# Grouped attention on one core: score columns laid out in whole PSUM banks, 12 score matmuls per group in place of 18

One core of one Trainium2 chip. The metric is the device time of one execution, in microseconds (us); the median of several executions is quoted.

## The reference

```python
B, Hq, Hkv, Sq, Sk, D = 16, 32, 8, 288, 512, 128          # bf16 inputs, values 0.05 * normal
k = jnp.repeat(k, Hq // Hkv, axis=1); v = jnp.repeat(v, Hq // Hkv, axis=1)
scores = jnp.einsum("bhqd,bhkd->bhqk", q, k) * D ** -0.5
p = softmax(scores, axis=-1)
out = jnp.einsum("bhqk,bhkd->bhqd", p, v)
```

Four query heads share one key/value head. The kernel treats each of the 16 x 8 = 128 pairs of batch and key head as a **group**: 4 x 288 = 1152 query rows are nine tiles of 128, and 512 keys are four tiles of 128, so a group has 36 score tiles of 128 x 128.

## The kernel before

A group is worked in three **chunks** of three query tiles, 1536 score columns each, three banks of PSUM. Two chunk buffers take turns (`ps_s`), the exponentials go to six buffers in SBUF (`pt_sb`). For chunk n TensorE computes scores, ScalarE takes the exponential without subtracting a maximum (a check at the end falls back to a general path), and TensorE multiplies chunk n-3's exponentials with V, to which a column of ones is appended that gives the row sums. VectorE divides. In every ninth chunk VectorE computes the last 120 columns of the exponential itself (a "shared" chunk).

```python
BANK, TPC = 512, 3                 # TPC: query tiles per chunk
CH = TPC * BANK                    # 1536
LAG, W, EVERY, FIRST_SHARED = 3, 120, 9, 4
TW = TPC * P                       # 384: one key tile's columns within a chunk

cuts = sorted(set(range(0, CH + 1, BANK)) | set(range(0, CH + 1, TW)))
pieces = [(c, c // TW, c % TW, e - c) for c, e in zip(cuts[:-1], cuts[1:])]   # 384,128,256,256,128,384

def op_s(n):                       # scores of chunk n
    g, i = n // NC, n % NC
    waits = [have("k", g), have_q(g, i)]
    if n >= 2:
        waits.append(("s_e", n - 1))              # exponential n-2 has freed the buffer
    qg = qt_sb[:, g % NQ, i * TPC:(i + 1) * TPC].rearrange("d t p -> d (t p)")
    for x, (c, j, r0, w) in enumerate(pieces):
        if shared(n) and c + w == CH:
            w -= W
        ... matmul(ps_s[:, n % 2, c:c + w], kt_sb[:, sl, j, gi, :], qg[:, r0:r0 + w])

def op_pv(r):                      # values of chunk r
    waits = [("s_vc", g + 1), ("s_e", r + 1)] ...
    for j in range(NJ):
        for a in range(TPC):
            ... matmul(outs(r)[:, a, :], pt_sb[:, r % NPT, j, a * P:(a + 1) * P], v_sb[...])

# TensorE:
for n in range(NS):                # NS = 384
    op_s(n)
    ...
    if n >= LAG:
        op_pv(n - LAG)
```

The start: the first group's queries come in three transposing loads of three tiles, the first K is loaded plainly, transposed by TensorE and copied in one piece; dummy matmuls fill TensorE's time until then.

Of the kernel before, what the change touches and what calls it, by code (L numbers as in the profile page):

```python
# [131 lines left out]
def bass_standalone__gqa_softmax__near_ridge_kernel(  # L132
# [8 lines left out]
    P = 128  # L141
# [20 lines left out]
    W = 120  # L162
    EVERY = 9
    NB = 2
    TW = TPC * P
    UG = 4
    NU = NG // UG
    NSLOT = 3
    NQ = 12
    NPT = 6  # L170
    WARM = 5
    FIRST_SHARED = 4
    AHEAD = 1.08
    NO = 12
    NS = NG * NC
# [10 lines left out]
    with ExitStack() as es:  # L186
# [20 lines left out]
            S("s_q%d" % i)  # L207
        for i in range(NO):
            S("s_o%d" % i)
        for i in range(NC):  # L210
            S("s_qp%d" % i)


# [24 lines left out]
        ident = main.enter_context(nc.sbuf_tensor("ident", [P, P], BF16))  # L238
        ones_b = main.enter_context(nc.sbuf_tensor("ones_b", [P, P], BF16))
        kt_sb = main.enter_context(nc.sbuf_tensor("kt_sb", [P, NSLOT, NJ, UG, P], BF16))  # L240
        pt_sb = main.enter_context(nc.sbuf_tensor("pt_sb", [P, NPT, NJ, TW], BF16))
        o_sb = main.enter_context(nc.sbuf_tensor("o_sb", [P, NO, NT, D], BF16))
        rl_sb = main.enter_context(nc.sbuf_tensor("rl_sb", [P, NG * NT], FP32))
        st_sb = main.enter_context(nc.sbuf_tensor("st_sb", [P, 2, B], FP32))
# [25 lines left out]
        def emit(eng, waits, fn):  # L270
            waits = need(eng, waits)
            for (s, n) in waits[:-1]:
                eng.wait_ge(s, n)
            ins = fn()
            if waits:
                ins.wait_op(waits[-1][0], waits[-1][1], "sem-ge")
            return ins
# [33 lines left out]

        def op_q0(i):

            c0, c1 = i * TPC, (i + 1) * TPC
            nc.sync.dma_start_transpose(qt_sb[:, 0, c0:c1], q_v[0:P, c0 * D:c1 * D]).then_inc(sem["s_qp%d" % i], 16)  # L315

        def have_q(g, i):
            if g == 0:
                return ("s_qp%d" % i, 16)
            return ("s_q%d" % (g % NQ), 16 * (g // NQ + (0 if g % NQ == 0 else 1)))  # L320

        def have(kind, g):

            u = g // UG
            if u == 0 and kind == "k":
                return ("s_k%d" % min(g, 2), (1, 1, 16)[min(g, 2)])
            if u == 0:
                return ("s_v%d" % (g // 2 * 2), 16)
            return ("us_%s%d" % (kind, u % NSLOT), 16 * (u // NSLOT + (0 if u % NSLOT == 0 else 1)))
# [16 lines left out]



        cuts = sorted(set(range(0, CH + 1, BANK)) | set(range(0, CH + 1, TW)))
        pieces = [(c, c // TW, c % TW, e - c) for c, e in zip(cuts[:-1], cuts[1:])]  # L350

        def op_kt(g, tiles, bank):

# [19 lines left out]
        def op_s(n):  # L373
            eng = nc.tensor
            g, i = n // NC, n % NC
            sl, gi = (g // UG) % NSLOT, g % UG
            waits = [have("k", g), have_q(g, i)]
            if n >= 2:
                waits.append(("s_e", n - 1))
            qg = qt_sb[:, g % NQ, i * TPC:(i + 1) * TPC].rearrange("d t p -> d (t p)")  # L380
            for x, (c, j, r0, w) in enumerate(pieces):
                if shared(n) and c + w == CH:
                    w -= W
                ins = emit(eng, waits if x == 0 else [], lambda: eng.matmul(  # L384
                    ps_s[:, n % 2, c:c + w], kt_sb[:, sl, j, gi, :], qg[:, r0:r0 + w], start=True, stop=True))
                if n == 0 and c + w == BANK:
                    ins.then_inc(sem["s_s0"], 1)
            ins.then_inc(sem["s_s"], 1)

        def op_sy(n):  # L390

            eng = nc.tensor
            g, t = n // NC, n % NC * TPC + TPC - 1
            emit(eng, [("s_ev", n - LAG - 1)], lambda: eng.matmul(  # L394
                ps_o[:, (n - LAG) % 2, BANK - W:BANK], kt_sb[:, (g // UG) % NSLOT, NJ - 1, g % UG, :],
                qt_sb[:, g % NQ, t, P - W:P], start=True, stop=True))

        def outs(r):

            if r == NS - 1:  # L400
                return ps_s[:, (NS - 2) % 2].rearrange("p (a e) -> p a e", e=BANK)[:, :, 0:DV]
            return ps_o[:, r % 2, 0:TPC * DV].rearrange("p (a e) -> p a e", e=DV)

        def op_pv(r):
            eng = nc.tensor
            g = r // NC
            sl, gi = (g // UG) % NSLOT, g % UG
            waits = [("s_vc", g + 1), ("s_e", r + 1)]
            if 2 <= r < NS - 1:
                waits.append(("s_ev", r - 1))  # L410


            for j in range(NJ):
                for a in range(TPC):
                    w_x = waits if a == 0 and j == 0 else []
                    if a == TPC - 1 and j == NJ - 1 and shared(r):
                        w_x = w_x + [("s_yp", nth(r))]
                    ins = emit(eng, w_x, lambda: eng.matmul(  # L418
                        outs(r)[:, a, :], pt_sb[:, r % NPT, j, a * P:(a + 1) * P],
                        v_sb[:, sl, gi * NJ + j, 0:DV], start=(j == 0 and a == 0), stop=(j == NJ - 1),  # L420
                        skip_group_check=True))
            ins.then_inc(sem["s_pv"], 1)

        def op_pv_last(a):

            eng = nc.tensor
            sl, gi = (LASTG // UG) % NSLOT, LASTG % UG
            for j in range(NJ):
                ins = emit(eng, [("s_e", NS + (0 if a < TPC - 1 else 1))], lambda: eng.matmul(
                    outs(NS - 1)[:, a, :], pt_sb[:, (NS - 1) % NPT, j, a * P:(a + 1) * P],  # L430
                    v_sb[:, sl, gi * NJ + j, 0:DV], start=(j == 0), stop=(j == NJ - 1)))
            if a == TPC - 1:
                ins.then_inc(sem["s_pv"], 1)


        def op_exp(n):
            eng = nc.scalar
            waits = [("s_s", n + 1)]
            if n >= NPT:
                waits.insert(0, ("s_pv", n - NPT + 1))  # L440
            dst, src = pt_sb[:, n % NPT], ps_s[:, n % 2].rearrange("p (j r) -> p j r", r=TW)
            parts = [(dst.rearrange("p j r -> p (j r)"), ps_s[:, n % 2])]
            if shared(n):
                parts = [(d[:, 0:CH - W], s[:, 0:CH - W]) for (d, s) in parts]
            if n == 0:
                d, s = parts[0]
                emit(eng, [("s_s0", 1)], lambda: eng.activation(d[:, 0:BANK], s[:, 0:BANK], ACTF.Exp, scale=scale))  # L447
                parts = [(d[:, BANK:CH], s[:, BANK:CH])]
            if n == NS - 1:
                w = TW - P  # L450
                parts = [(dst[:, :, 0:w], src[:, :, 0:w]), (dst[:, :, w:TW], src[:, :, w:TW])]
            for (d, s) in parts:
                emit(eng, waits, lambda: eng.activation(d, s, ACTF.Exp, scale=scale)).then_inc(sem["s_e"], 1)  # L453


        def shared(n):
            return FIRST_SHARED <= n < NS - 6 and (n - FIRST_SHARED) % EVERY == 0

        def nth(n):
            return (n - FIRST_SHARED) // EVERY + 1  # L460

# [27 lines left out]

        def op_yp(n):  # L490
            eng, b = nc.vector, nth(n) % NB
            emit(eng, [("s_pv", n - NPT + 1), ("s_ym", 2 * nth(n)), ("s_yu", 3 * nth(n))],
                 lambda: eng.scalar_tensor_tensor(  # L493
                     out=pt_sb[:, n % NPT, NJ - 1, TW - W:TW], in0=u_sb[:, b, 2], scalar=QUARTIC[3],
                     in1=e_sb[:, b].bitcast(FP32), op0=ALU.add, op1=ALU.mult)).then_inc(sem["s_yp"], 1)


# [62 lines left out]
                op0=ALU.is_lt, op1=ALU.add)).then_inc(sem["s_bad"], 1)  # L560


        first = [lambda i=i: op_q0(i) for i in range(NC)]
        first += [lambda: op_q(1), lambda: op_k(0, 2), lambda: op_q(2), lambda: op_v(0, None, 2, UG), lambda: op_q(3)]

        sp = []
# [21 lines left out]
        @block.tensor  # L588
        def _(eng):
            op_warm(WARM, BANK, ps_o[:, 1])  # L590
            op_kt(0, range(NJ), 0)
            op_warm(8, P, ps_s[:, 1])
            for n in range(NS):
                if n == 2:
                    op_warm(4, P, ps_o[:, 0])
                op_s(n)
                if shared(n):
                    op_sy(n)
                if n == 2:
                    op_kt(1, range(NJ), 1)  # L600
                if n >= LAG:
                    op_pv(n - LAG)
            for r in range(NS - LAG, NS - 1):
                op_pv(r)
            for a in range(TPC):
                op_pv_last(a)
            emit(eng, [("s_ev", NS - 1), ("s_bad", 2)], lambda: eng.matmul(  # L607
                ps_o[0:1, NS % 2, 0:ALONE + 1], one_f[:], bad_sb[:, 1, :], start=True, stop=True)
            ).then_inc(sem["s_bad"], 1)
            choose(eng, "pe")  # L610
# [26 lines left out]
        def _(eng):  # L637
            eng.memset(z_sb[:], 0.0).then_inc(sem["s_z"], 1)  # L638
            eng.memset(dum[:], 0.0).then_inc(sem["s_one"], 1)
            eng.memset(one_f[:], 1.0)  # L640
            op_kc(0, range(NJ), 0, 1)
            op_kc(1, range(NJ), 1, 2)
            per_b = G * NC
            w0 = NS - 1 - ALONE // TPC
            last = rl_sb[:, NG * NT - ALONE:NG * NT]
# [62 lines left out]
```

## Time and profile before

| | before |
|---|---|
| time, median | 525.38 us (525.32 to 526.12, 3 runs) |
| span in the profile | 523.5 us |
| TensorE busy, ScalarE busy | 99%, 98% |
| score matmuls, value matmuls per chunk | 6, 12 |
| chunk on TensorE | 1.335 us |
| chunk on ScalarE, when it is not kept waiting | 1.343 us, shared one 1.243 us |

In a line of a group of instructions, the numbers after the bar are busy time in us, mean duration of one in ns, and the engine's idle time before them. In the timeline the first two numbers are start and duration in us.

One ruler is used: **the time from the end of the fourth exponential to the end of the last full one**, 379 chunks later. It leaves out start and tail, and its two ends can be read from two lines of ScalarE's timeline. For the kernel before, the first line is among those of the prediction (9.92 + 1.45); the second is

```profile
516.00 1.50 ACT L453 ACTIVATE pt_sb<-ps_s 128x1536 bf16<-128x1536 f32 x1
```

In ns the ends are 11.373 and 517.506: 506.13 us. Behind the second end there are 6.02 us of tail.

### The profile page before, as it was taken

Reading aid. Unit: us, or ns where it says so; the run is one execution under the profiler, and the core shown is the slowest. Engines: PE = TensorE matmul, PEld = TensorE weight load, DVE = VectorE, ACT = ScalarE, POOL = GpSimd, SP = SyncE. Lnnn points to the kernel's source line nnn. Section 1 sums busy time; section 2 is a strip of 40 time slices with the busy share of each in tenths; the row PEclk is TensorE's granted clock in tenths of the full one; section 3 lists DMA queues with packets and bytes.
Section 4 is the critical chain, followed back from the end, with each engine's and each line's share of the span. In section 5 each row is a group of like instructions: output and inputs, shape, how many; then the busy total and the mean of one; then the engine's idle time right before and its main releaser. Section 6 shows DMA issues by size and latency. Waiting matters only on the chain.

```text
span 523.5 us, 16876 instructions
## 1 busy us (share of the span) xinstructions
PE 517.6 (99%) x6981; PEld 459.0 (88%) x6981; DVE 339.9 (65%) x1148; ACT 515.1 (98%) x389; POOL 79.6 (15%) x135
## 2 busy tenths in 40 slices
PE   7999999999999999999999999999999999999997
PEld 5888888888888888888888888888888888888886
DVE  2766666666666666666666666666666666666665
ACT  6999999999999999999999999999999999999996
POOL 1111111111111111111111111111111111111110
PEclk9999999999999999999999999999999999999999
DMA  8999999999999999999999999999988999896212
GB/s 167 223 255 246 205 223 252 194 205 245 252 196 275 208 211 248 215 225 219 216 228 221 222 203 252 230 184 246 225 218 211 233 211 201 219 212 178 79 69 92
DMA packets 253147, 110.15 MB, mean 210 GB/s; under 512 B 219792, under 2 KB 236816, under 8 KB 253072
## 3 DMA queue, kind: packets, MB, share of 16 engines
q1 hardware_dynamic: 252512, 108.56, 97.7%
q8 instruction: 55, 0.90, 0.7%
q10 hardware_dynamic: 560, 0.52, 0.4%
q14 instruction: 20, 0.16, 0.1%
HBM read 17.04 MB, written 37.75 MB: 105 GB/s over the span
## 4 chain that ended last, share of the span: by engine, by line
PE 97%; DMA 1%; SPq 1%; DVE 0%; issue 0%
PE ps_o L418 50%; PE ps_s L384 47%; DMA qt_sb<-in_q_dram 1%; SPq L315 1%; PE ps_o L394 0%; DVE o_sb L522 0%; DVE rl_sb L512 0%; DVE o_sb L532 0%; PE ps_o L607 0%; DVE bad_sb L558 0%; DVE flag_i L675 0%; DVE bad_sb L555 0%
## 5 line engine op out<-in xcount | busy, mean ns | idle before, releaser
L453 ACT ACTIVATE pt_sb<-ps_s 128x1536 bf16<-128x1536 f32 (+2 forms) x385 | 512.8, 1455 | 0.6 <-PE ps_s L384 0.5
L418 PE MATMUL ps_o<-v_sb,pt_sb 128*128 128x129 bf16 x4596 | 322.8, 220 | 0.2 <-DVE o_sb L522 0.2
L384 PE MATMUL ps_s<-qt_sb,kt_sb 128*128 128x128 bf16 (+3 forms) x2304 | 312.2, 272 | 1.5 <-DMA qt_sb<-in_q_dram 1.4
L418 PEld LDWEIGHTS ps_o<-v_sb,pt_sb 128*128 128x128 bf16 x4596 | 289.9, 98 | 22.9 <-DVE o_sb L522 0.4
L384 PEld LDWEIGHTS ps_s<-qt_sb,kt_sb 128*128 128x128 bf16 x2304 | 193.4, 98 | 35.6 <-issue 1.0
L522 DVE TENSOR_TENSOR o_sb<-ps_o,rl_sb 128x384 bf16<-128x384 f32 x383 | 212.9, 556 | 10.3
L512 DVE RECIPROCAL rl_sb<-ps_o 128x3 f32<-128x3 f32 x383 | 68.7, 179 | 160.8 <-PE ps_o L418 160.8
L505 POOL COPY v_sb<-vd_sb 128x512 bf16<-128x512 bf16 x128 | 78.7, 615 | 431.6 <-PE ps_o L418 412.2
L486 DVE SCALAR_TENSOR_TENSOR u_sb<-u_sb,m_sb 128x120 f32<-128x120 f32 x84 | 23.4, 278 | 0.0
L493 DVE SCALAR_TENSOR_TENSOR pt_sb<-u_sb,e_sb 128x120 bf16<-128x120 f32 x42 | 12.2, 290 | 1.4
L486 DVE SCALAR_TENSOR_TENSOR u_sb<-m_sb 128x120 f32<-128x120 f32 x42 | 11.6, 277 | 0.0
L464 DVE TENSOR_SCALAR y_sb<-ps_o 128x120 f32<-128x120 f32 x42 | 10.6, 253 | 0.0
L477 DVE TENSOR_SCALAR m_sb<-t_sb 128x120 int32<-128x120 int32 x42 | 9.4, 223 | 1.4
L477 DVE TENSOR_SCALAR e_sb<-t_sb 128x120 int32<-128x120 int32 x42 | 9.5, 226 | 0.0
L394 PE MATMUL ps_o<-qt_sb,kt_sb 128*128 128x120 bf16 x42 | 9.1, 216 | 0.0
L470 DVE TENSOR_SCALAR t_sb<-y_sb 128x120 int32<-128x120 f32 x42 | 9.0, 213 | 0.0
L364 DVE COPY kt_sb<-ps_o 128x512 bf16<-128x512 bf16 x2 | 0.8, 424 | 6.6 <-PE ps_o L357 6.6
L394 PEld LDWEIGHTS ps_o<-qt_sb,kt_sb 128*128 128x128 bf16 x42 | 4.1, 98 | 0.0
L370 PE MATMUL ps_o<-z_sb 128*128 128x512 bf16 (+1 forms) x9 | 2.7, 447 | 1.3 <-DVE z_sb L638 1.3
L548 DVE TENSOR_REDUCE st_sb<-rl_sb 128x1 f32<-128x72 f32 (+1 forms) x16 | 3.5, 217 | 0.0
L550 DVE TENSOR_REDUCE st_sb<-rl_sb 128x1 f32<-128x72 f32 (+1 forms) x16 | 3.5, 216 | 0.0
L447 ACT ACTIVATE pt_sb<-ps_s 128x512 bf16<-128x512 f32 x1 | 0.6, 597 | 2.3 <-PE ps_s L384 2.3
(31 smaller groups left out, 11.6 us busy)
## 6 DMA issues: line engine op xcount, KB each, us to landing
out_dram<-o_sb SPq DMA_DIRECT2D x127, 288.0 KB, 4.0
vd_sb<-in_v_dram SPq DMA_DIRECT2D x31, 512.0 KB, 5.3
qt_sb<-in_q_dram SPq DMA_TRANSPOSE x130, 4.8
kt_sb<-in_k_dram SPq DMA_TRANSPOSE x32, 5.2
out_dram<-o_sb SPq DMA_DIRECT2D x3, 96.0 KB, 1.8
kd_sb<-in_k_dram ACTq DMA_DIRECT2D x2, 128.0 KB, 2.2
vd_sb<-in_v_dram ACTq DMA_DIRECT2D x1, 256.0 KB, 3.0
vd_sb<-in_v_dram SPq DMA_DIRECT2D x1, 256.0 KB, 3.4
```

The source lines that it names most:

```text
L384: ins = emit(eng, waits if x == 0 else [], lambda: eng.matmul(ps_s[:, n % 2, c:c + w], kt_sb[:, sl, j, gi, :], qg[:, r0:r0 + w], start=Tru ...
L394: emit(eng, [("s_ev", n - LAG - 1)], lambda: eng.matmul(ps_o[:, (n - LAG) % 2, BANK - W:BANK], kt_sb[:, (g // UG) % NSLOT, NJ - 1, g % UG, :],
L418: ins = emit(eng, w_x, lambda: eng.matmul(outs(r)[:, a, :], pt_sb[:, r % NPT, j, a * P:(a + 1) * P], v_sb[:, sl, gi * NJ + j, 0:DV], start ...
L453: emit(eng, waits, lambda: eng.activation(d, s, ACTF.Exp, scale=scale)).then_inc(sem["s_e"], 1)
L464: emit(eng, [("s_yb", nth(n) - NB), ("s_pv", n - LAG + 1)], lambda: eng.tensor_scalar(out=y_sb[:, b], in0=ps_o[:, (n - LAG) % 2, BANK - W: ...
L470: emit(eng, [("s_ym", 2 * (nth(n) - NB)), ("s_y", nth(n))], lambda: eng.tensor_scalar(out=t_sb[:, b], in0=y_sb[:, b], scalar1=Y_MUL, scala ...
L477: emit(eng, [("s_yp", nth(n) - NB), ("s_yb", nth(n))], lambda: eng.tensor_scalar(out=dst[:, b], in0=t_sb[:, b], scalar1=mask, scalar2=bits ...
L486: lambda: eng.scalar_tensor_tensor(out=u_sb[:, b, x], in0=src, scalar=QUARTIC[x], in1=m, op0=ALU.add, op1=ALU.mult)
L493: lambda: eng.scalar_tensor_tensor(out=pt_sb[:, n % NPT, NJ - 1, TW - W:TW], in0=u_sb[:, b, 2], scalar=QUARTIC[3], in1=e_sb[:, b].bitcast( ...
L505: emit(eng, waits, lambda: eng.tensor_copy(v_sb[:, sl, gi * NJ:(gi + 1) * NJ, 0:D], vd_sb[:, sl, gi].rearrange("p (j d) -> p j d", d=D))). ...
L512: emit(eng, [("s_pv", r + 1)], lambda: eng.reciprocal(rl_sb[:, TPC * r:TPC * (r + 1)].unsqueeze(2), outs(r)[:, :, D:DV])).then_inc(sem["s_ ...
L522: emit(eng, waits, lambda: eng.tensor_tensor(out=o_sb[:, g % NO, t0:t0 + TPC, :], in0=outs(r)[:, :, 0:D], in1=rl_sb[:, TPC * r:TPC * (r + ...
```

## The change

The intent is to spend fewer matmuls on the same score columns. Instead of three query tiles against four key tiles within a chunk, a bank now holds one key tile against four query tiles. Eight query tiles give eight whole banks, and the ninth query tile against all four key tiles fills a ninth bank. So a group has 8 matmuls of 512 columns and 4 of 128, none cut at a bank's border. A query tile's probabilities then lie in two chunks, and the waits of the value matmuls follow. Chunk 0 needs four query tiles, so the first group's queries come in two loads (4 and 5 tiles); K's first tile is copied ahead of the other three.

```diff
-    TW = TPC * P
+    TB = BANK // P
+    NF = NT // TB * TB
-    FIRST_SHARED = 4
+    FIRST_SHARED = 6
...
-            c0, c1 = i * TPC, (i + 1) * TPC
+            c0, c1 = ((0, TB), (TB, NT))[i]
             nc.sync.dma_start_transpose(qt_sb[:, 0, c0:c1], ...)
...
-        cuts = sorted(set(range(0, CH + 1, BANK)) | set(range(0, CH + 1, TW)))
-        pieces = [(c, c // TW, c % TW, e - c) for c, e in zip(cuts[:-1], cuts[1:])]
+        def place(t, j):
+            b, c = (t // TB * NJ + j, t % TB * P) if t < NF else (NF // TB * NJ + t - NF, j * P)
+            return b // TPC, b % TPC * BANK + c
+        def pieces(i):
+            left = [(place(t, j)[1], j, t, TB * P) for t in range(0, NF, TB) for j in range(NJ) if place(t, j)[0] == i]
+            return left + [(place(t, j)[1], j, t, P) for t in range(NF, NT) for j in range(NJ) if place(t, j)[0] == i]
+        def uses(b):      # the last chunk that value chunk b reads
+            return max(place(t, j)[0] for t in range(b * TPC, (b + 1) * TPC) for j in range(NJ))
...
+                if n == 0 and x < 2:
+                    w_x = [("s_k0", 1), waits[1]] if x == 0 else waits[:1]
...
-            waits = [("s_vc", g + 1), ("s_e", r + 1)]
+            waits = [("s_vc", g + 1), ("s_e", g * NC + uses(r % NC) + 1)]
...
-            op_kt(0, range(NJ), 0)
-            op_warm(8, P, ps_s[:, 1])
+            op_kt(0, range(1), 0)
+            op_kt(0, range(1, NJ), 1)
+            op_warm(5, P, ps_s[:, 1])
```

Cut: the same re-indexing in the value matmuls, the last exponential, VectorE's 120 columns and their extra matmul, and the second copy of K.

More of the change, by code (lines that the diff above doesn't have):

```diff
@@ L209, in bass_standalone__gqa_softmax__near_ridge_kernel @@
             S("s_o%d" % i)
-        for i in range(NC):
+        for i in range(2):
             S("s_qp%d" % i)
@@ L240, in bass_standalone__gqa_softmax__near_ridge_kernel @@
         kt_sb = main.enter_context(nc.sbuf_tensor("kt_sb", [P, NSLOT, NJ, UG, P], BF16))
-        pt_sb = main.enter_context(nc.sbuf_tensor("pt_sb", [P, NPT, NJ, TW], BF16))
+        pt_sb = main.enter_context(nc.sbuf_tensor("pt_sb", [P, NPT, CH], BF16))
         o_sb = main.enter_context(nc.sbuf_tensor("o_sb", [P, NO, NT, D], BF16))
@@ L318, in have_q @@
             if g == 0:
-                return ("s_qp%d" % i, 16)
+                return ("s_qp%d" % min(i, 1), 16)
             return ("s_q%d" % (g % NQ), 16 * (g // NQ + (0 if g % NQ == 0 else 1)))
@@ L325, in have @@
             if u == 0 and kind == "k":
-                return ("s_k%d" % min(g, 2), (1, 1, 16)[min(g, 2)])
+                return ("s_k%d" % min(g, 2), (2, 1, 16)[min(g, 2)])
             if u == 0:
@@ L345, in stored, with used, pt @@
             return [("s_o%d" % (g % NO), 16 * (g // NO + 1)) for g in range(NG - NO, LASTG)] + [("s_ol", 16 * NC)]
-        cuts = sorted(set(range(0, CH + 1, BANK)) | set(range(0, CH + 1, TW)))
-        pieces = [(c, c // TW, c % TW, e - c) for c, e in zip(cuts[:-1], cuts[1:])]
+        def place(t, j):
[6 more added lines that the diff above has]
+            return max(place(t, j)[0] for t in range(b * TPC, (b + 1) * TPC) for j in range(NJ))
+        def used(i):
+            return max(b for b in range(NC) for t in range(b * TPC, (b + 1) * TPC) for j in range(NJ) if place(t, j)[0] == i)
+        def pt(g, t, j):
+            i, c = place(t, j)
+            return pt_sb[:, (g * NC + i) % NPT, c:c + P]
         def op_kt(g, tiles, bank):
@@ L379, in op_s @@
                 waits.append(("s_e", n - 1))
-            qg = qt_sb[:, g % NQ, i * TPC:(i + 1) * TPC].rearrange("d t p -> d (t p)")
-            for x, (c, j, r0, w) in enumerate(pieces):
+            qg = qt_sb[:, g % NQ].rearrange("d t p -> d (t p)")
+            todo = pieces(i)
+            for x, (c, j, t, w) in enumerate(todo):
                 if shared(n) and c + w == CH:
                     w -= W
-                ins = emit(eng, waits if x == 0 else [], lambda: eng.matmul(
-                    ps_s[:, n % 2, c:c + w], kt_sb[:, sl, j, gi, :], qg[:, r0:r0 + w], start=True, stop=True))
+                w_x = waits if x == 0 else []
+                if n == 0 and x < 2:
+                    w_x = [("s_k0", 1), waits[1]] if x == 0 else waits[:1]
+                ins = emit(eng, w_x, lambda: eng.matmul(
+                    ps_s[:, n % 2, c:c + w], kt_sb[:, sl, j, gi, :], qg[:, t * P:t * P + w], start=True, stop=True))
                 if n == 0 and c + w == BANK:
@@ L392, in op_sy @@
             eng = nc.tensor
-            g, t = n // NC, n % NC * TPC + TPC - 1
+            g = n // NC
+            (t, j), = [(t, j) for t in range(NT) for j in range(NJ) if place(t, j) == (n % NC, CH - P)]
             emit(eng, [("s_ev", n - LAG - 1)], lambda: eng.matmul(
-                ps_o[:, (n - LAG) % 2, BANK - W:BANK], kt_sb[:, (g // UG) % NSLOT, NJ - 1, g % UG, :],
+                ps_o[:, (n - LAG) % 2, BANK - W:BANK], kt_sb[:, (g // UG) % NSLOT, j, g % UG, :],
                 qt_sb[:, g % NQ, t, P - W:P], start=True, stop=True))
@@ L415, in op_pv @@
                     w_x = waits if a == 0 and j == 0 else []
-                    if a == TPC - 1 and j == NJ - 1 and shared(r):
-                        w_x = w_x + [("s_yp", nth(r))]
+                    t = r % NC * TPC + a
+                    i, c = place(t, j)
+                    if c == CH - P and shared(g * NC + i):
+                        w_x = w_x + [("s_yp", nth(g * NC + i))]
                     ins = emit(eng, w_x, lambda: eng.matmul(
-                        outs(r)[:, a, :], pt_sb[:, r % NPT, j, a * P:(a + 1) * P],
+                        outs(r)[:, a, :], pt(g, t, j),
                         v_sb[:, sl, gi * NJ + j, 0:DV], start=(j == 0 and a == 0), stop=(j == NJ - 1),
@@ L429, in op_pv_last @@
                 ins = emit(eng, [("s_e", NS + (0 if a < TPC - 1 else 1))], lambda: eng.matmul(
-                    outs(NS - 1)[:, a, :], pt_sb[:, (NS - 1) % NPT, j, a * P:(a + 1) * P],
+                    outs(NS - 1)[:, a, :], pt(LASTG, NT - TPC + a, j),
                     v_sb[:, sl, gi * NJ + j, 0:DV], start=(j == 0), stop=(j == NJ - 1)))
@@ L439, in op_exp @@
             if n >= NPT:
-                waits.insert(0, ("s_pv", n - NPT + 1))
-            dst, src = pt_sb[:, n % NPT], ps_s[:, n % 2].rearrange("p (j r) -> p j r", r=TW)
-            parts = [(dst.rearrange("p j r -> p (j r)"), ps_s[:, n % 2])]
+                m = n - NPT
+                waits.insert(0, ("s_pv", m // NC * NC + used(m % NC) + 1))
+            d, s = pt_sb[:, n % NPT], ps_s[:, n % 2]
+            parts = [(0, CH)]
             if shared(n):
-                parts = [(d[:, 0:CH - W], s[:, 0:CH - W]) for (d, s) in parts]
+                parts = [(0, CH - W)]
             if n == 0:
-                d, s = parts[0]
                 emit(eng, [("s_s0", 1)], lambda: eng.activation(d[:, 0:BANK], s[:, 0:BANK], ACTF.Exp, scale=scale))
-                parts = [(d[:, BANK:CH], s[:, BANK:CH])]
+                parts = [(BANK, CH)]
             if n == NS - 1:
-                w = TW - P
-                parts = [(dst[:, :, 0:w], src[:, :, 0:w]), (dst[:, :, w:TW], src[:, :, w:TW])]
+                parts = [(0, CH - BANK), (CH - BANK, CH)]
+            parts = [(d[:, a:e], s[:, a:e]) for (a, e) in parts]
             for (d, s) in parts:
@@ L491, in op_yp @@
             eng, b = nc.vector, nth(n) % NB
-            emit(eng, [("s_pv", n - NPT + 1), ("s_ym", 2 * nth(n)), ("s_yu", 3 * nth(n))],
+            emit(eng, [("s_pv", (n - NPT) // NC * NC + used((n - NPT) % NC) + 1), ("s_ym", 2 * nth(n)), ("s_yu", 3 * nth(n))],
                  lambda: eng.scalar_tensor_tensor(
-                     out=pt_sb[:, n % NPT, NJ - 1, TW - W:TW], in0=u_sb[:, b, 2], scalar=QUARTIC[3],
+                     out=pt_sb[:, n % NPT, CH - W:CH], in0=u_sb[:, b, 2], scalar=QUARTIC[3],
                      in1=e_sb[:, b].bitcast(FP32), op0=ALU.add, op1=ALU.mult)).then_inc(sem["s_yp"], 1)
@@ L560, in op_over @@
                 op0=ALU.is_lt, op1=ALU.add)).then_inc(sem["s_bad"], 1)
-        first = [lambda i=i: op_q0(i) for i in range(NC)]
+        first = [lambda i=i: op_q0(i) for i in range(2)]
         first += [lambda: op_q(1), lambda: op_k(0, 2), lambda: op_q(2), lambda: op_v(0, None, 2, UG), lambda: op_q(3)]
@@ L640, in _ @@
             eng.memset(one_f[:], 1.0)
-            op_kc(0, range(NJ), 0, 1)
-            op_kc(1, range(NJ), 1, 2)
+            op_kc(0, range(1), 0, 1)
+            op_kc(0, range(1, NJ), 1, 2)
+            op_kc(1, range(NJ), 1, 3)
             per_b = G * NC
```

## The prediction

> **What bounds the kernel now.** I read the page's busy shares first, then the costliest groups, then the chain that ended last, and at last single instructions, because the first three cannot separate two engines that are both full.
>
> ```profile
> PE 517.6 (99%) x6981; PEld 459.0 (88%) x6981; DVE 339.9 (65%) x1148; ACT 515.1 (98%) x389; POOL 79.6 (15%) x135
> L453 ACT ACTIVATE pt_sb<-ps_s 128x1536 bf16<-128x1536 f32 (+2 forms) x385 | 512.8, 1455 | 0.6 <-PE ps_s L384 0.5
> L418 PE MATMUL ps_o<-v_sb,pt_sb 128*128 128x129 bf16 x4596 | 322.8, 220 | 0.2 <-DVE o_sb L522 0.2
> L384 PE MATMUL ps_s<-qt_sb,kt_sb 128*128 128x128 bf16 (+3 forms) x2304 | 312.2, 272 | 1.5 <-DMA qt_sb<-in_q_dram 1.4
> ```
>
> TensorE and ScalarE are both busy for 98 to 99% of the span, and neither waits: ScalarE's exponentials sat idle 0.6 us in all, the score matmuls 1.5 us, the value matmuls 0.2 us. The work is 384 chunks of 1536 score columns (128 groups of 3). The chain of waits in a quiet stretch shows TensorE alone, running through:
>
> ```profile
> 80.00 0.66 PE ps_s L384 x6
> 80.66 0.68 PE ps_o L418 x12
> 81.33 0.66 PE ps_s L384 x6
> 81.99 0.68 PE ps_o L418 x12
> ```
>
> So a chunk costs TensorE 0.655 + 0.680 = 1.335 us (the first number from the records in ns, which the view rounds to 0.66). TensorE sets the pace. How far behind it is ScalarE? Single exponentials from the timeline of that engine (start, duration):
>
> ```profile
> 86.05 1.44 ACT L453 ACTIVATE pt_sb<-ps_s 128x1536 bf16<-128x1536 f32 x1
> 94.06 1.49 ACT L453 ACTIVATE pt_sb<-ps_s 128x1536 bf16<-128x1536 f32 x1
> 95.39 1.40 ACT L453 ACTIVATE pt_sb<-ps_s 128x1416 bf16<-128x1416 f32 x1
> 96.72 1.45 ACT L453 ACTIVATE pt_sb<-ps_s 128x1536 bf16<-128x1536 f32 x1
> ```
>
> The first two are six chunks apart. Starts: 8.01 us, so 1.335 each: TensorE's pace. Ends: 87.491 to 95.551 in ns, 8.060 us, so 1.343 each. The starts are released by TensorE, but each end slips 8 ns further behind, and the recorded duration grows from 1.444 to 1.494 us. ScalarE's own pace is thus 1.343 us, slower than TensorE's. The third line is every ninth chunk, in which VectorE computes 120 columns instead: its end comes 1.243 us after the one before, which repays the slip, and the next one's end comes 1.374 us later, so ScalarE starved there for 31 ns, once in nine chunks. Per nine chunks TensorE takes 12.017 us (start of one shared chunk to the next), ScalarE needs 8 x 1.3433 + 1.243 = 11.990 us. **ScalarE has only 0.027 us of slack in 12.017, 0.2%.** That number decides the case.
>
> DMA shows 97.7% of its engines' time, but the load of the queries for group 10 landed 6.8 us before its first use, for group 60 23 us, for group 120 38 us: loads get ahead all the time, and nothing waits for them after 9.1 us.
>
> **What the Trainium skill says.** "TensorE: Matmul & The Clock Gate", section "Back-to-back issue gap", gives an isolated gap of N/2.4 + 2.5 ns at full clock. The trace agrees: six score matmuls hold 1536 columns, 640 ns at 2.4 GHz, and took 655, so 2.5 ns each. "ScalarE: Activation LUTs", section "What ACT_TABLE_LOAD costs", says 186 ns + 0.833 N for an ACTIVATE with immediates, back-to-back ones overlapping by about 93 ns; that would be 1466 ns alone and 1373 sustained. The trace has a mean of 1467 for a full one, but 1343 sustained, so 63 ns over the 1280 of its columns; I use the trace's. "PSUM — Partial Sum Buffer", section "The four PSUM rules", says a matmul's output stays within one bank: that is why 384-column tiles over 512-column banks made six pieces of four, and why bank-sized pieces need no cuts.
>
> **The change, part by part.**
>
> (a) Score matmuls. A group's 36 tiles were 18 matmuls (per chunk 384, 128, 256, 256, 128, 384) and become 8 of 512 and 4 of 128. The columns stay the same, 4608. Six matmuls fewer at 2.5 ns is 15 ns a group, 5 ns a chunk, and 768 x 2.5 ns = 1.9 us in all. Weight loads go from 18 to 12, but the score matmuls' loads (98 ns) already lie under the stream (the value matmuls have one each 56.7 ns), so they give nothing more. TensorE would go to 1.330 us a chunk and 12.017 - 0.045 = 11.972 per nine.
>
> (b) That is below ScalarE's 11.990. **The bound moves to ScalarE**, whose columns, instructions and 42 shared chunks (first one 6 instead of 4, still every ninth) are unchanged. Of the 45 ns per nine, 27 can be had. From the fourth to the last full exponential the ends are 506.13 us apart; ScalarE's own need is 379 x 1.3434 - 42 x 0.1004 = 504.95. Gain: 1.18 us.
>
> (c) Dependencies. A value chunk now needs up to the exponential two after the score chunk it was paired with: the first third of a group needs two chunks, the other two all three. But value chunk n-3 is issued behind score chunk n, and that already waits for exponential n-2, the latest it can now need. Nothing new is waited for in the steady part. VectorE's 120 columns are now used in the following value chunk: more slack, not less.
>
> (d) The start. The views of it:
>
> ```profile
> 4.62 1.74 PE L384 MATMUL ps_s<-qt_sb,kt_sb 128*128 128x384 bf16 x12
> 7.16 0.81 PE L384 MATMUL ps_s<-qt_sb,kt_sb 128*128 128x384 bf16 x6 [0.58 <-DMA qt_sb<-in_q_dram]
> 9.07 0.81 PE L384 MATMUL ps_s<-qt_sb,kt_sb 128*128 128x384 bf16 x6 [0.87 <-DMA qt_sb<-in_q_dram]
> 9.92 1.45 ACT L453 ACTIVATE pt_sb<-ps_s 128x1536 bf16<-128x1536 f32 x1 [0.46 <-PE ps_s L384]
> 0.82 3.90 SPq L315 DMA_TRANSPOSE qt_sb<-in_q_dram  x3
> 4.77 1.43 SPq L310 DMA_TRANSPOSE qt_sb<-in_q_dram  x1
> ```
>
> Three query loads took 1.3 us of issue each; then the second group's load was issued at 4.77, landed at 8.94 and held up the fourth score chunk, so ScalarE stood still for 0.46 us. With two loads it is issued at about 3.5. Its packets then fall where the third load's began (5.4 us, in the trace's packets), nine tiles took 1.5 us and 0.85 to 1.25 more to land: about 8.0 to 8.3. Against that, the second load now has five tiles; three landed at 5.49, at about 0.2 to 0.3 us a tile five land at 5.9 to 6.2. Score chunk 1 then starts near 6.05 (was 5.53), its exponential 0.87 later, at 6.9 (was 6.44); then ScalarE runs without a break: 8.3, and the fourth at 9.65 instead of 9.92. The first exponential moves from 5.04 to about 4.8 (K in two copies, five dummy matmuls instead of eight), which is hidden behind that second load. Gain: 0.27 us, between 0.1 and 0.5.
>
> (e) The end. Now the last value chunks follow TensorE. With ScalarE as the bound TensorE runs ahead as far as two score buffers let it: its last chunks come about 0.25 us nearer to the last exponential (end of the full one at 517.51, last matmul of value chunk 380 at 517.75 before; an estimate from 0.06 us release, 0.65 scores, 0.68 values). The last but one value chunk now needs the first part of the last exponential, but waits longer anyway for VectorE's eviction (0.36 us). Gain about 0.25 us.
>
> Sum: 1.18 + 0.27 + 0.25 = 1.7 us, 525.4 - 1.7 = **523.7 us**, 0.3% faster.
>
> **The rivals.** First, TensorE stays the bound, with the whole 1.9 us of (a) and some 0.8 us of the earlier fourth score chunk: 522.7. For it: the chain names TensorE for 97%. Against it: the slip of 8 ns per chunk and the 31 ns of starvation say that ScalarE cannot follow. Second, the wait that takes its place costs more than it saves: once ScalarE is the bound, each score chunk waits for exponential n-2 to free its buffer, and if this stop and restart cost 10 ns a chunk, 3.8 us are lost: about 527. Against it: from release to the next exponential's readiness takes 0.06 + 0.87 us, and ScalarE needs it only 1.23 us after, so 0.3 us are spare, also for the shared chunk's 0.1. Third, the larger second load delays the start by more than I think, the fourth exponential comes no sooner or 0.3 later: 524.0 to 524.3. Against it: packets of the same nine tiles must pass in either case.
>
> **Range and chances.** The rivals span 522.7 to 527, and the runs of before spread over 0.8 us. Range 522.8 to 525.1. Two per cent is 10.5 us; no part of the change touches so much. Faster by over 2%: 0.01; within 2%: 0.98; slower: 0.01.
>
> **What would show it.** (a): twelve score matmuls a group, at 0.650 us a chunk when not waiting. (b): ends of full exponentials 1.343 apart throughout and none at 1.374 after a shared one; a nine-chunk period of 11.99; small waits of the score matmuls for exponentials. With a period of 11.97 the first rival holds, above 12.0 the second. (d): landing of the second load near 6.0, of the next group's near 8.2, the fourth exponential at 9.65. I am wrong if ScalarE's 1.343 us is not its limit, or if the release of the buffers leaves bubbles on it.

## The result

The changed kernel takes **523.41 us** (523.31 to 523.83, 4 runs); before now 525.69 us (525.32 to 526.12, 4 runs). The ratio of the two is 0.9958 (95% interval 0.9941 to 0.9975). A ratio here is the mean time of one kernel's fast runs over that of the other's of the same rounds, so not quite the ratio of the medians. The time lies within the predicted range and 0.3 us below the predicted point.

The page of the changed kernel, the same lines as those of before:

```profile
PE 511.6 (98%) x6104; PEld 394.5 (76%) x6210; DVE 339.5 (65%) x1149; ACT 513.9 (98%) x389; POOL 79.4 (15%) x135
L481 ACT ACTIVATE pt_sb<-ps_s 128x1536 bf16<-128x1536 f32 (+2 forms) x385 | 511.5, 1683 | 0.6 <-PE ps_s L409 0.6
L446 PE MATMUL ps_o<-v_sb,pt_sb 128*128 128x129 bf16 x4596 | 322.9, 220 | 0.1
L409 PE MATMUL ps_s<-qt_sb,kt_sb 128*128 128x512 bf16 (+2 forms) x1430 | 295.9, 322 | 6.2 <-DVE kt_sb L385 0.6
```

Three of these numbers mislead. The 1430 score matmuls are 1536; 106 records are missing from this trace, and a later run of the same kernel has them all. That also makes TensorE look less busy. And an exponential seems to have grown by 16%, from 1455 to 1683 ns, while the kernel got faster. Single exponentials from ScalarE's timeline tell what that is:

```profile
149.57 1.68 ACT L481 ACTIVATE pt_sb<-ps_s 128x1536 bf16<-128x1536 f32 x1
156.22 1.74 ACT L481 ACTIVATE pt_sb<-ps_s 128x1536 bf16<-128x1536 f32 x1
157.55 1.66 ACT L481 ACTIVATE pt_sb<-ps_s 128x1416 bf16<-128x1416 f32 x1
158.88 1.67 ACT L481 ACTIVATE pt_sb<-ps_s 128x1536 bf16<-128x1536 f32 x1
```

The first two are five chunks apart. Their starts are 6.650 us apart, 1.330 a chunk, TensorE's new pace; their ends, 151.246 and 157.962, 6.716 us, 1.343 a chunk. The third is a shared one: its end (159.205) comes 1.243 later and the next end (160.549) 1.344 after that. In the kernel before that last step was 1.374: ScalarE starved there. **It starves no more.** The recorded starts keep TensorE's pace and so follow the scores, not the work, and the duration counts waiting in line; in this trace an exponential starts up to 0.417 us before its predecessor has ended. The ends show the work: among the steps between full exponentials none is outside 1.342 to 1.345 us. (In two later profiles, `again` and one_copy, one step is longer: 1.393 us behind the first shared chunk; after it none.)

The chain of waits, the same view as in the prediction:

```profile
80.91 0.65 PE ps_s L409 x3
81.56 0.68 PE ps_o L446 x12
...
83.57 0.66 PE ps_s L409 x6
84.22 0.68 PE ps_o L446 x12
```

Three score matmuls of 512, or two of 512 and four of 128, in place of six. The chain still names TensorE for 98% of the span, although ScalarE now sets the pace: TensorE's stalls are too short for this view, as the pair every18 and before18 below shows.

The ruler:

```profile
9.94 1.46 ACT L481 ACTIVATE pt_sb<-ps_s 128x1536 bf16<-128x1536 f32 x1
514.59 1.73 ACT L481 ACTIVATE pt_sb<-ps_s 128x1536 bf16<-128x1536 f32 x1
```

In ns the ends are 11.396 and 516.320, **504.92 us** (predicted: 504.95; before: 506.13). The tail is 5.78 us (before 6.02). The fourth exponential itself came no sooner. So the span's gain of 523.53 - 522.10 = 1.43 us is 1.21 from the ruler, 0.24 from the tail, -0.02 from the start. The profiled execution was the slowest of four (523.83 us); the medians lie some 2 us apart.

The start of the changed kernel, from the timelines of TensorE, ScalarE and the loads:

```profile
8.89 0.81 PE L409 MATMUL ps_s<-qt_sb,kt_sb 128*128 128x512 bf16 x3 [0.56 <-DVE kt_sb L385]
7.26 4.13 ACT L481 ACTIVATE pt_sb<-ps_s 128x1536 bf16<-128x1536 f32 x3 [0.37 <-PE ps_s L409]
0.82 2.64 SPq L316 DMA_TRANSPOSE qt_sb<-in_q_dram  x2
3.51 1.48 SPq L311 DMA_TRANSPOSE qt_sb<-in_q_dram  x1
```

The second group's queries were issued at 3.51 instead of 4.77 us, as meant, but the fourth score chunk began at 8.89 instead of 9.07 only, and what it waited for last was the copy of the second group's K. In this profile that is not what set the fourth exponential. The second line shows three exponentials without a break from 7.26 us on, and the fourth is the last of them: their ends, 8.711, 10.054 and 11.396, are ScalarE's own pace. What came late is the first of the three, which the prediction had at 6.9: the three score matmuls of its chunk took 402 to 427 ns each, since TensorE's clock was released at 7.10 us only.

### The profile page after: what moved, and what is told of

Read it like the earlier page. It is cut to its first block, busy times and chain, and to the rows that moved or that the text cites. A ratio compares the mean times of both kernels' runs of the same rounds, so it can differ in the third digit from the quotient of the medians.

```text
span 522.1 us, 15059 instructions
## 1 busy us (share of the span) xinstructions
PE 511.6 (98%) x6104; PEld 394.5 (76%) x6210; DVE 339.5 (65%) x1149; ACT 513.9 (98%) x389; POOL 79.4 (15%) x135
## 4 chain that ended last, share of the span: by engine, by line
PE 98%; issue 1%; DVE 1%
PE ps_o L446 50%; PE ps_s L409 47%; PE ps_o L391 0%; PE ps_o L420 0%; DVE o_sb L550 0%; PE ps_o L378 0%; PE ps_s L391 0%; DVE rl_sb L540 0%; DVE kt_sb L385 0%; DVE o_sb L560 0%; DVE z_sb L667 0%; PE ps_o L636 0%; DVE bad_sb L586 0%; DVE flag_i L705 0%; DVE bad_sb L583 0%
## 5 line engine op out<-in xcount | busy, mean ns | idle before, releaser
L481 ACT ACTIVATE pt_sb<-ps_s 128x1536 bf16<-128x1536 f32 (+2 forms) x385 | 511.5, 1683 | 0.6 <-PE ps_s L409 0.6
L446 PEld LDWEIGHTS ps_o<-v_sb,pt_sb 128*128 128x128 bf16 x4596 | 284.6, 98 | 53.2 <-DVE o_sb L550 0.3
L409 PE MATMUL ps_s<-qt_sb,kt_sb 128*128 128x512 bf16 (+2 forms) x1430 | 295.9, 322 | 6.2 <-DVE kt_sb L385 0.6
L409 PEld LDWEIGHTS ps_s<-qt_sb,kt_sb 128*128 128x128 bf16 x1536 | 118.3, 98 | 62.9 <-DMA qt_sb<-in_q_dram 0.8
```

Of the source, the lines that this page charges most:

```text
L409: ins = emit(eng, w_x, lambda: eng.matmul(ps_s[:, n % 2, c:c + w], kt_sb[:, sl, j, gi, :], qg[:, t * P:t * P + w], start=True, stop=True))
L446: ins = emit(eng, w_x, lambda: eng.matmul(outs(r)[:, a, :], pt(g, t, j), v_sb[:, sl, gi * NJ + j, 0:DV], start=(j == 0 and a == 0), stop=( ...
L481: emit(eng, waits, lambda: eng.activation(d, s, ACTF.Exp, scale=scale)).then_inc(sem["s_e"], 1)
```

## The experiments

The main theory: before, TensorE is the bound with ScalarE 0.2% behind; the change takes 2.5 ns for each of 768 matmuls from TensorE, whereupon ScalarE is the bound. Rivals: TensorE is still the bound; the bank layout helps by itself; the gain comes from the new start.

All kernels gave correct results. Each was timed against the kernel before on the same chip, so the ratios are to be compared.

| kernel | score matmuls a group | shared chunks | 4th end, us | ruler, us | tail, us | mean exp, ns | median, us | ratio to before |
|---|---|---|---|---|---|---|---|---|
| before | 18 | 42 | 11.37 | 506.13 | 6.02 | 1460 | 525.38 | |
| before_again | 18 | 42 | 11.52 | 505.99 | 6.03 | 1463 | 525.27 (1 run, state unknown) | |
| start_only | 18 | 42 | 11.29 | 506.11 | 6.02 | 1461 | 525.12 | 0.9995 |
| before18 | 18 | 21 | 11.55 | 507.11 | 5.78 | 1687 | 526.21 | 1.0018 |
| changed | 12 | 42 | 11.40 | 504.92 | 5.78 | 1690 | 523.41 | 0.9958 |
| again | 12 | 42 | 11.24 | 504.97 | 5.79 | 1656 | 523.60 | 0.9973 |
| one_copy | 12 | 42 | 11.38 | 504.97 | 5.78 | 1656 | 523.73 | 0.9966 |
| every18 | 12 | 21 | 11.22 | 507.07 | 5.78 | 1717 | 525.76 | 1.0005 |
| every6 | 12 | 62 | 11.36 | 504.15 | 5.97 | 1455 | 523.04 | 0.9954 |
| every6_b | 12 | 62 | 10.98 | 504.34 | 5.97 | 1449 | 523.02 | 0.9954 |
| early | 12 | 62 | 10.94 | 504.34 | 5.97 | 1449 | 523.18 | 0.9969 |
| split | 20 | 42 | 11.23 | 506.56 | 6.06 | 1457 | 525.56 | 1.0002 |

The mean durations leave out the first six and the last two records of exponentials. Six runs are enough to meet an odd one: `again` has one of 525.94 us and `early` one of 526.81, 2.4 and 3.7 us above the median of the rest of their kernel; `before18` and the kernel before had such runs too (527.04, 526.42). The record gives a granted clock of 0.997 for the first two, against 0.999 to 1.000 for all other runs, the smaller two included. No profile caught one and its cause stays open. They are why the ratios of `again` and `early` are higher than their medians suggest.

### again: the changed kernel once more

No edit.

> The changed kernel once more, unaltered, to learn how much the first microseconds vary. Theory (ScalarE is the bound from the second chunk on, and the start depends on when TensorE's clock is released): ends of the 4th to the last full exponential again 504.9 us apart, none starved; the 4th exponential's end near 10.8 us if the clock is released before 5.7 us, near 11.4 us if it is released near 7.1 us as in the first profile; time 523.0 to 523.9. Rival (the late 4th exponential is due to the loads, not to the clock): its end at 11.4 us whatever the clock does.

The ruler came out at 504.97 us, the time at 523.60. TensorE's clock was released to full speed at 5.75 us in this profile (7.10 in the first), and the fourth exponential, still held up by TensorE, ended at 11.24 us:

```profile
9.79 1.45 ACT L481 ACTIVATE pt_sb<-ps_s 128x1536 bf16<-128x1536 f32 x1 [0.22 <-PE ps_s L409]
```

That is a miss for my explanation of the start: I had expected 10.8 us with an earlier clock. The clock is worth 0.15 us, not 0.6. In this run the score chunk began at 8.95, with the second group's queries landed at 8.81: a load stands behind it. The rival, that the clock makes no difference at all, is not right either.

### every6 and every6_b: relieve ScalarE

```diff
-    EVERY = 9
+    EVERY = 6
```

> The changed kernel with every sixth chunk shared instead of every ninth: 62 shared chunks in place of 42, so ScalarE has 20 x 0.100 = 2.0 us less to do and TensorE 20 matmuls of 2.5 ns more. Theory (ScalarE is the bound of the changed kernel, TensorE close behind at 1.330 us a chunk): ends of the 4th to the last full exponential fall from 504.9 to 504.2 us and TensorE is the bound again, with starving after each shared chunk; the tail behind the last full exponential grows back by some 0.2 us; time lower by 0.3 to 0.6 us than the changed kernel. Rival (TensorE is the bound of the changed kernel): no gain, 0.05 us slower.

> The changed kernel with every sixth chunk shared once more, to compare with on the same chip: 522.9 to 523.2 us, ends of the 4th to the last full exponential 504.2 us.

The ruler fell to 504.15 us (504.34 in the second run), as expected, and the time to 523.04 (523.02). The ruler's lines, and then the same three neighbours around a shared chunk:

```profile
9.90 1.46 ACT L481 ACTIVATE pt_sb<-ps_s 128x1536 bf16<-128x1536 f32 x1
513.97 1.54 ACT L481 ACTIVATE pt_sb<-ps_s 128x1536 bf16<-128x1536 f32 x1
```

```profile
156.08 1.48 ACT L481 ACTIVATE pt_sb<-ps_s 128x1536 bf16<-128x1536 f32 x1
157.41 1.39 ACT L481 ACTIVATE pt_sb<-ps_s 128x1416 bf16<-128x1416 f32 x1
158.72 1.45 ACT L481 ACTIVATE pt_sb<-ps_s 128x1536 bf16<-128x1536 f32 x1
```

The starving is back: the third ends 1.369 us after the second, and durations are again near 1.45. TensorE is the bound, at 379 x 1.330 + 62 x 0.0027 = 504.2 us, just where its own sum puts it. Taking 2.0 us from ScalarE gained 0.6 to 0.8 on the ruler, because TensorE stood that close behind. Less work for ScalarE made the changed kernel faster, so TensorE was not its bound.

### every18 and before18: the same burden on both kernels

```diff
-    EVERY = 9
+    EVERY = 18
```

in the changed kernel (every18) and in the kernel before (before18): 21 shared chunks fewer, 21 x 0.1004 = 2.1 us more for ScalarE.

> The changed kernel with every 18th chunk shared: 21 in place of 42, ScalarE has 2.1 us more. Theory (ScalarE is the bound): all of it shows, ends 507.0 us apart instead of 504.9, time higher by 2.1 us, near 525.5. Rival (TensorE is the bound): hidden, no change beyond 0.2 us.

> The kernel before with every 18th chunk shared: 21 in place of 42, ScalarE has 2.1 us more to do. Theory (ScalarE had 1.2 us of slack in the kernel before and is then the bound): ends of the 4th to the last full exponential 507.0 us apart, the same as in the changed kernel with 21 shared chunks, so only 0.9 of the 2.1 us show there; with a tail shorter by 0.24 us the time is near 526.1. Rival (ScalarE was as much the bound before): all 2.1 us, 527.5.

The fourth and the last full exponential (the fourth ended at 11.215 and 11.546 us), first of every18, then of before18:

```profile
9.77 1.45 ACT L481 ACTIVATE pt_sb<-ps_s 128x1536 bf16<-128x1536 f32 x1 [0.17 <-PE ps_s L409]
516.51 1.77 ACT L481 ACTIVATE pt_sb<-ps_s 128x1536 bf16<-128x1536 f32 x1
```

```profile
10.10 1.45 ACT L453 ACTIVATE pt_sb<-ps_s 128x1536 bf16<-128x1536 f32 x1
516.89 1.76 ACT L453 ACTIVATE pt_sb<-ps_s 128x1536 bf16<-128x1536 f32 x1
```

The rulers are 507.07 and 507.11 us. Two kernels with 12 and with 18 score matmuls a group take the same time as soon as ScalarE bounds both, and it is ScalarE's own sum, 379 x 1.3434 - 21 x 0.1004 = 507.04. The changed kernel shows all 2.1 us of the burden, the kernel before only 1.0 to 1.1: the other 1.0 to 1.2 went into the slack that the prediction had read from eight nanoseconds a chunk. **This pair settles the cause.**

It also shows where TensorE's waits are. The waits view lists none of the score matmuls for exponentials. In the records, though, the step from the first to the second score matmul of a chunk, otherwise 216 ns for 512 columns and 163 for 384, is some 10 ns longer in 192 places of every18 (1.9 us in all, counting only those of 8 ns or more), in 28 places of `again`, there from 182 us on, in 54 of before18, in none of before and of every6. These are waits for the buffer which exponential n-2 frees. The first score matmul of chunk n carries that wait. In all these places its recorded start is 55 to 59 ns after the end of exponential n-2, and from chunk 5 on no chunk of these three kernels starts sooner than that; in every6 it starts 147 ns or more after it, in before 310 or more. So the buffer holds TensorE back where ScalarE is the bound and nowhere else.

### split: the layout without the saving

```diff
-            left = [(place(t, j)[1], j, t, TB * P) for t in range(0, NF, TB) for j in range(NJ) if place(t, j)[0] == i]
+            left = [(place(t, j)[1] + x * P, j, t + x, TB // 2 * P) for t in range(0, NF, TB) for j in range(NJ)
+                    if place(t, j)[0] == i for x in (0, TB // 2)]
```

The condition for K's second copy moves to the third matmul with it.

> The changed kernel with each score matmul of 512 columns cut into two of 256, same layout, same loads: 20 score matmuls a group instead of 12 (before: 18). Theory (the gain is the fixed cost of 2.5 ns per matmul and nothing else about the layout): scores of a chunk 0.657 us, a chunk 1.337 us, TensorE the bound again; ends of the 4th to the last full exponential 506.7 us apart; time some 2.0 us above the changed kernel, near 525.4. Rival (the bank-by-bank layout itself is what helps): stays within 0.3 us of the changed kernel.

```profile
9.77 1.46 ACT L482 ACTIVATE pt_sb<-ps_s 128x1536 bf16<-128x1536 f32 x1
516.31 1.48 ACT L482 ACTIVATE pt_sb<-ps_s 128x1536 bf16<-128x1536 f32 x1
```

506.56 us (expected 506.7), 525.56 us in time: the bank-by-bank layout with 20 matmuls is no faster than the old one with 18 (506.13). In the records a matmul of 128 columns holds the stream for 55.8 ns on average, one of 256 for 109.2, and in every6 one of 512 for 215.8: that is 0.4166 ns for a column and 2.5 ns for each matmul. The number of matmuls is what counts, and the layout by itself gives nothing.

### start_only and one_copy: the start alone, and a part of it undone

start_only puts the new start on the old layout:

```diff
-            c0, c1 = i * TPC, (i + 1) * TPC
+            c0, c1 = ((0, 4), (4, NT))[i]
-            op_kt(0, range(NJ), 0)
-            op_warm(8, P, ps_s[:, 1])
+            op_kt(0, range(1), 0)
+            op_kt(0, range(1, NJ), 1)
+            op_warm(5, P, ps_s[:, 1])
```

and the waits and copies that belong to it. one_copy undoes the copies and dummy matmuls in the changed kernel.

> The kernel before with the changed start alone (queries of the first group in two loads of 4 and 5 tiles, first K in two copies, five dummy matmuls), its old score layout kept. Theory (TensorE still needs 1.335 us a chunk and sets the pace; the fourth score chunk starts near 8.9 us in place of 9.07 because the second group's queries and K come hardly sooner): ends of the 4th to the last full exponential 506.1 us apart, the 4th one's end 11.2 to 11.4 us, time 525.1 to 525.5, no gain to speak of. Rival (the new start is where the gain comes from): 523.5 to 524.0.

> The changed kernel with K's first copy undone (one transposed K of four tiles in one copy, eight dummy matmuls). Theory (the second query load, not the first score piece, sets when ScalarE runs on): first exponential 5.0 to 5.3 us, the 4th one's end still 11.2 to 11.6 us, ends to the last 504.9 us; time within 0.3 us of the changed kernel. Rival (the two copies earn their part): 0.3 to 0.5 us slower.

start_only: ruler 506.11 us, time 525.12. Its last full exponential:

```profile
515.89 1.50 ACT L456 ACTIVATE pt_sb<-ps_s 128x1536 bf16<-128x1536 f32 x1
```

It ended at 517.40 against 517.51 us, and its fourth score chunk began at 8.96 against 9.07: the same 0.11 us, which is all that the start gives; the ratio of 0.9995 (0.9978 to 1.0012) cannot show so little. one_copy: the first exponential starts 0.4 us later (5.40 against 5.01), the fourth ends at 11.38, the time is 523.73 us with a ratio of 0.9966 against 0.9973 and 0.9958 of the changed kernel. So nothing was lost, but not for the reason that I had given. The first exponential is later than expected (5.0 to 5.3). In this profile the second query load had landed at 5.24 us, before it was needed, and the second score chunk, at 6.01, ran straight behind the first (in the first profile of the changed kernel it began at 5.76, just behind that load's landing at 5.71). What hid the later start is the fourth score chunk, which began at 9.08 with the second group's queries landed at 8.95.

### before_again: the kernel before, another release of the clock

No edit.

> The kernel before, unaltered, for a second profile of its start with another moment of the clock's release. Theory (its fourth score chunk waits for the second group's queries, whatever the clock): the 4th exponential's end at 11.3 to 11.5 us; ends to the last 506.1 us. Rival (its start in the first profile was lucky, with the clock released at 4.5 us): end later than 11.6 us if the clock comes at 6 to 7 us.

The clock came at 7.07 us this time instead of 4.54. The fourth exponential ended at 11.52 instead of 11.37, but the last full one at 517.51 in both: the fourth score chunk began at 9.07 in both, its queries having landed at 8.94, and in the kernel before it is TensorE that counts from there. Compared at the same late clock, the changed kernel's fourth exponential is 0.12 us earlier (11.396 against 11.516).

### early: a version aimed at the start

On top of every sixth chunk shared:

```diff
+                if n == 1 and x < 2:
+                    w_x = [] if x == 0 else waits
-                if n == 2:
+                if n == 1:
                     op_kt(1, range(NJ), 1)
```

> Every sixth chunk shared, and two moves in the start: the first matmul of the second score chunk no longer waits for the second query load (its queries came with the first), and the second group's K is transposed after the second score chunk instead of the third. Theory (TensorE is the bound with 62 shared chunks, so the time moves with the start of the fourth score chunk, which waits for the second group's queries to land at 8.4 to 8.8 us and for that K): fourth score chunk at 8.5 to 8.9 us in place of 8.87 to 8.95, ends of the 4th to the last full exponential 504.2 us; time 0 to 0.35 us below the kernel with every sixth chunk shared alone, near 522.8. Rival (the start is limited by ScalarE's own first three exponentials): no change.

The second group's K was ready at 7.44 instead of 8.46 us (every6_b, same chip), the fourth score chunk began at 8.64 instead of 8.68, and the time did not change (523.18 and 523.02 us). The queries landed at 8.51 and 8.55: with the copy of K out of the way, that landing is what is left, and the fourth exponential (9.49) stands close behind the third as well: it ended 1.355 us after it, 12 ns over ScalarE's own pace. So the rival's outcome, no change. The fastest version is the changed kernel with every sixth chunk shared, twice 523.0 us at a ratio of 0.9954 (0.9941 to 0.9967). On the chip that ran both, it was 0.56 us below the changed kernel by the medians, 523.04 and 523.60.

## Why the prediction was right

- **(a) The saving on TensorE.** Right. Scores of a chunk take 0.65 us on average; split put matmuls back at the same price, and the time of before came back.
- **(b) The bound moves to ScalarE, which caps the gain at 1.18 us.** Right, 1.21 measured. (The prediction's sum 379 x 1.3434 - 42 x 0.1004 is 504.93, not 504.95, so its cap should read 1.20.) The pair every18 and before18 shows the cap directly. The nine-chunk period is 11.990 us as forecast (shared ends at 159.205 and 171.195).
- **(c) No new wait in the steady part.** Right as far as the trace shows it: full exponentials end 1.342 to 1.345 us apart from the fourth on. Where the prediction says that a value chunk needs up to the exponential "two after", the code has one after: value chunk n-3 needs exponential n-2 at the latest, as its next sentence says. And its "nothing waits" for loads after 9.1 us holds for the queries: GpSimd's copies of V waited three more times, up to 34.8 us, though the value matmuls sat idle 0.2 us in all.
- **(d) The start, 0.27 us.** Mis-sized: 0.11 us (start_only) to 0.12 (same clock). Two terms failed. The first is the landing of the second group's queries, "about 8.0 to 8.3": it was 8.36 to 8.95 us in the nine profiles with the new loads, and in `again` it held up the fourth score chunk and with it the fourth exponential. (The second load, forecast "near 6.0", landed at 5.24 to 6.10.) I had let its packets end where the free stretch allowed, but the load of V, issued from the other queue at about 3.4, now landed at 7.2 to 7.5 in eight of the nine (8.7 in one_copy) instead of 6.3 to 6.5, so the loads shared their engines for longer; that this sharing is the reason is argued, not shown. Besides, I overlooked that the fourth score chunk also needs the second group's K, copied by 8.33 to 8.84 (early aside). The second term is the 0.87 us from the second score chunk's start to its exponential. It was 1.50 us in the first profile (5.76 to 7.26), where the clock was released at 7.10, and about 1.0 in `again` (5.80 to 6.78), where it was released at 5.75. With the late release ScalarE ran on from 7.26 without a break, and that, not the queries, set the fourth exponential. The prediction did not reckon with the moment of the release.
- **(e) The tail, 0.25 us.** Right: 0.24. It goes with the bound and not with the layout: before18 has 5.78 us and the changed kernel too, split has 6.06.

Of the rivals, TensorE as the lasting bound would have needed a gain of nothing in every6; the costly stop and restart did not come, since a wait of 10 ns behind a buffer with 0.3 us to spare starves nobody.

The sum of the profiled spans is 1.43 us instead of 1.7, the medians differ by 2.0 us or, in the second session, 1.8; all of them are inside what such runs scatter. So it is in part luck that 523.41 lies so near to 523.7: the forecast gain of the start did not show in the pair of first profiles (-0.02 us), and the medians' scatter filled the gap. The ruler is the firmer evidence.

## What to carry to other kernels

Where two engines are both at 98%, look at the pace of each by the ends of its instructions: the one whose ends slip behind its starts has its own pace, and the difference is all that a change on the other engine can earn. Work it out before the change, in ns per period, and rebalance with the change (here: every sixth instead of every ninth chunk shared), or the rest of the saving is lost. Here a mean duration that grew while ends kept their pace was queueing, and in these runs it told which of the two is the bound: 1449 to 1463 ns with TensorE as the bound, 1656 to 1717 with ScalarE.

## What the Trainium skill lacked or had wrong

- "ScalarE: Activation LUTs", section "What ACT_TABLE_LOAD costs": back-to-back ACTIVATEs overlap by about 93 ns, which with its cost for immediate operands would make an estimated 1373 ns for 1536 columns. From PSUM to SBUF these runs give 1343 (1243 for 1416 columns): 63 ns over the columns' time. That the prediction's mean of 1467 fits the 1466 for one alone is no confirmation: the same full exponentials are recorded with 1444 to 1502 ns in that profile, the wait in line included.
- "Perfetto Trace Analysis", section "Per-instruction lifecycle: what the profiler-reported window actually captures": the recorded start of a ScalarE instruction is the moment at which it begins executing. Here starts lie up to 0.417 us before the predecessor's end while the ends keep a fixed pace, so recorded durations hold queueing time.
- "TensorE: Matmul & The Clock Gate", section "Back-to-back issue gap": its sustained figures, about 81 ns at N=128 and 131 at N=512, do not fit; the stream here, with a weight load per matmul, holds 56 and 216 ns, as the isolated formula has it. The same page, section "What you observe", lets the clock's release vary by 500 ns either way from run to run; these runs vary by more: the changed kernel had it at 5.75 and 7.10 us, the kernel before at 4.54 and 7.07, each with its dummy matmuls from 1.27 us on.
